# Chunked attention and a squared-ReLU feed-forward on one core: transposes of q, k and of the attention output by DMA instead of by TensorE

## The chip, the cores and the metric

The kernel runs on one core of a Trainium2 chip. A core has five engines with a queue of instructions each: TensorE (PE, with its weight loads as PEld), VectorE (DVE), ScalarE (ACT), GpSimd (POOL) and SyncE (SP), which here issues all DMAs. 16 DMA engines do the transfers. The metric is the device time of one execution in microseconds (us); lower is better.

## The reference

Attention within chunks of 64 tokens, and then a feed-forward layer over all tokens. B = 8, H = 8 heads, S = 576, D = 64, so 4608 tokens of 512 features; d_ff = 2048.

```
q_c, k_c, v_c = (t.reshape(B, H, S // 64, 64, D) for t in (q, k, v))
scores = D ** -0.5 * q_c @ k_c.transpose(0, 1, 2, 4, 3)
attn   = exp(scores - max); attn = attn / (sum(attn) + 1e-09)
x      = (attn @ v_c), heads side by side          # 4608 x 512
h      = maximum(x @ w_in, 0)                       # 4608 x 2048
out    = (h * h) @ w_out                            # 4608 x 512, float32
```

## The kernel before

The tokens are cut into 18 groups of 256, and the groups into 9 blocks: block 0 is groups 0 to 2, blocks 1 to 7 are two groups each (3 and 4, then 5 and 6, up to 15 and 16), block 8 is group 17 alone. q, k and v arrive from HBM as float32; a DMA for q or k brings 128 tokens with 8 heads, in pieces of 256 B. The matmuls take bf16.

For one group the attention has four steps, each a function:

- `transpose_qk` (T): TensorE transposes q (8 pieces of 128x128) and then k (8 more), L139, reading the upper halves of the float32 words as bf16. Both halves lie in one PSUM tile `ps_att`; DVE copies q's half to `qkT` (L146) and ACT copies k's half (L148).
- `scores` (SC): 64 matmuls of two groups (32 of one) at L160, then ACT's exponential (L167).
- `values` (AV): matmuls with v and a column of ones (L179); DVE takes the reciprocal of the sums (L186) and writes the normalized `x` in bf16 (L189), 128 tokens at a time.
- `transpose_x` (XT): TensorE transposes x (8 pieces, L205) and DVE copies the result to `xT` (L209).

`ffn_in` has 16 steps for a block: four matmuls (L224) into a bank of `ps_ffn`, ACT's relu (L230), DVE's square into `gT` (L231). `ffn_out` has 16 matmuls (L240) for each 128 tokens, ACT's copy to one of four `o_sb` buffers (L247) and a store (L249). `ps_ffn` has four banks and `ps_att` two.

The order is written by hand. The feed-forward of block j yields after each step of `ffn_in` and after every fourth matmul of `ffn_out`; each yield is a slot, 32 in a block of two groups. A plan puts the attention of block j+1 in slots of block j: T in slots 1 and 4, SC of both groups in 9, AV in 14 and 18, XT in 22 and 26. The loads of block j+2 (L85 for q and k, L97 and L104 for v) are issued on SP at the start of block j. Every queue runs in this order, so an instruction that waits on SP holds all later loads and stores.

Of the kernel before, what the change touches and what calls it, by code (L numbers as in the profile page):

```python
# [10 lines left out]
BF16 = mybir.dt.bfloat16  # L11
# [5 lines left out]
def kernel(  # L17
# [9 lines left out]
    nc = tc.nc  # L27

    B, H, S, D = q.shape
# [4 lines left out]
    n_hp = H // 2  # L34
    n_dt = d_model // 128
    n_ft = d_ff // 128
    GT = 256
    n_grp = n_tokens // GT
    blocks = [[0, 1, 2]] + [[g, g + 1] for g in range(3, n_grp - 1, 2)] + [[n_grp - 1]]
    BT = GT * max(len(b) for b in blocks)  # L40

    const_pool = ctx.enter_context(tc.tile_pool(name="const", bufs=1))
# [3 lines left out]
    att_pool = ctx.enter_context(tc.tile_pool(name="att", bufs=3))  # L46
# [20 lines left out]
    def segments(g0, n):  # L67
        while n:
            b, s = divmod(g0, S)
            m = min(n, S - s)  # L70
            yield b, s, m
            g0 += m
            n -= m

    qk = {}

    def load_qk(g):
        q_sb = in_pool.tile([128, 2, H, D], FP32, name="q_sb")
        k_sb = in_pool.tile([128, 2, H, D], FP32, name="k_sb")
        qk[g] = (q_sb, k_sb)  # L80
        for t in range(2):
            for dst, src in ((q_sb, q), (k_sb, k)):
                p = 0
                for b, s, m in segments(g * GT + t * 128, 128):
                    nc.sync.dma_start(  # L85
                        out=dst[p:p + m, t, :, :],
                        in_=src[b, :, s:s + m, :].rearrange("h s d -> s h d"))
                    p += m
# [19 lines left out]
    def load_w_in(i):  # L108
        cols = slice(i * 256, (i + 1) * 256)
        st = wst_pool.tile([128, 1024], FP32, name="w_st").rearrange("p (a f) -> p a f", a=n_dt)  # L110
        nc.sync.dma_start(  # L111
            out=st, in_=moe_w_in[:, cols].rearrange("(a p) f -> p a f", p=128))
        nc.gpsimd.tensor_copy(out=w_in_bf[:, :, cols], in_=st)  # L113
# [8 lines left out]
    xTs = {}  # L122
# [4 lines left out]
    state = {}  # L127

    def transpose_qk(g):
        ps = ps_att.tile([128, 1024], FP32, name="ps_att")  # L130
        psb = ps.bitcast(BF16)
        qkT = att_pool.tile([128, 2, n_hp, GT], BF16, name="qkT")
        state["qkT", g] = qkT
        for which in range(2):
            srcb = qk[g][which].bitcast(BF16)
            for hp in range(n_hp):
                for i in range(2):
                    c0 = which * 1024 + hp * GT + i * 128
                    nc.tensor.transpose(  # L139
                        out=psb[:, c0:c0 + 128],  # L140
                        in_=srcb[:, i, 2 * hp:2 * hp + 2, 1::2],
                        identity=ident)
            dst = qkT[:, which]
            src = psb[:, which * 1024:(which + 1) * 1024].rearrange("c (h t) -> c h t", h=n_hp)
            if which == 0:
                nc.vector.tensor_copy(out=dst, in_=src)  # L146
            else:
                nc.scalar.copy(out=dst, in_=src)  # L148

    def scores(g):  # L150
        qkT = state.pop(("qkT", g))
        ps = ps_att.tile([128, 1024], FP32, name="ps_att")
        for hp in range(n_hp):
            for t in range(2):
                for a in range(2):
                    for p in range(2):
                        c = p ^ a
                        cols = slice(t * 128 + p * 64, t * 128 + p * 64 + 64)
                        o0 = a * 512 + hp * 128 + t * 64
                        nc.tensor.matmul(  # L160
                            out=ps[64 * c:64 * c + 64, o0:o0 + 64],
                            lhsT=qkT[64 * a:64 * a + 64, 1, hp, cols],
                            rhs=qkT[64 * a:64 * a + 64, 0, hp, cols],
                            start=True, stop=True)
        e = att_pool.tile([128, 2, n_hp, 2, 64], BF16, name="e")
        state["e", g] = e
        nc.scalar.activation(  # L167
            out=e.rearrange("p a h t q -> p (a h t q)"), in_=ps, func=AF.Exp, scale=scale)
# [26 lines left out]
    def transpose_x(g):  # L195
        j, c = place[g]
        if j not in xTs:
            xTs[j] = att_pool.tile([128, n_dt, BT], BF16, name="xT", bufs=2)
        ps = ps_att.tile([128, 1024], FP32, name="ps_att")
        psb = ps.bitcast(BF16)  # L200
        for t in range(2):
            x = state.pop(("x", g, t))
            for hp in range(n_hp):
                c0 = hp * GT + t * 128
                nc.tensor.transpose(  # L205
                    out=psb[:, c0:c0 + 128],
                    in_=x[:, hp].rearrange("p a d -> p (a d)"),
                    identity=ident)
        nc.vector.tensor_copy(  # L209
            out=xTs[j][:, :, c:c + GT],  # L210
            in_=psb[:, 0:1024].rearrange("p (h t) -> p h t", h=n_hp))

    T, SC, AV, XT = transpose_qk, scores, values, transpose_x

    gTs = {}

    def ffn_in(j, c, n):
        if j not in gTs:
            gTs[j] = ffn_pool.tile([128, n_ft, BT], BF16, name="gT")
        gT, xT = gTs[j], xTs[j]  # L220
        for ft in range(n_ft):
            h = ps_ffn.tile([128, 512], FP32, name="ps_ffn")
            for dt in range(n_dt):
                nc.tensor.matmul(  # L224
                    out=h[:, 0:n],
                    lhsT=w_in_bf[:, dt, ft * 128:(ft + 1) * 128],
                    rhs=xT[:, dt, c:c + n],
                    start=(dt == 0), stop=(dt == n_dt - 1))
            rl = ffn_pool.tile([128, 512], BF16, name="rl", bufs=3)
            nc.scalar.activation(out=rl[:, 0:n], in_=h[:, 0:n], func=AF.Relu)  # L230
            nc.vector.tensor_tensor(  # L231
                out=gT[:, ft, c:c + n], in0=rl[:, 0:n], in1=rl[:, 0:n], op=ALU.mult)
            yield

    def ffn_out(j):
        gT = gTs.pop(j)
        for tt in range(len(blocks[j]) * GT // 128):
            o_ps = ps_ffn.tile([128, d_model], FP32, name="ps_ffn")
            for ft in range(n_ft):
                nc.tensor.matmul(  # L240
                    out=o_ps,
                    lhsT=gT[:, ft, tt * 128:(tt + 1) * 128],
                    rhs=w_out_bf[:, ft, :],
                    start=(ft == 0), stop=(ft == n_ft - 1))
                if ft == n_ft - 1:
                    o_sb = ffn_pool.tile([128, d_model], FP32, name="o_sb", bufs=4)
                    nc.scalar.copy(out=o_sb, in_=o_ps)  # L247
                    t0 = blocks[j][0] * GT + tt * 128
                    nc.sync.dma_start(out=out[t0:t0 + 128, :], in_=o_sb)  # L249
                if ft % 4 == 3:  # L250
                    yield

    def load(g):
        load_qk(g)
        load_v(g)

    load(0)
    load(1)
    load_w_in(0)
    load_w_in(1)  # L260
    load(2)
    for i in range(2, 8):
# [10 lines left out]
    for j, grps in enumerate(blocks):  # L273
        if j + 2 < len(blocks):
            for g in blocks[j + 2]:
                load(g)
        nxt = blocks[j + 1] if j + 1 < len(blocks) else []
        if j == 0:
            a, b = nxt
            plan = {3: [(T, 2)], 6: [(SC, 2)], 10: [(AV, 2)], 14: [(XT, 2)],  # L280
                    44: [(T, a)], 46: [(T, b)], 48: [(SC, a), (SC, b)],
                    50: [(AV, a)], 52: [(AV, b)], 54: [(XT, a)], 55: [(XT, b)]}
            phases = [ffn_in(0, 0, 512), ffn_in(0, 512, 256), ffn_out(0)]
        else:
            if len(nxt) == 2:
                a, b = nxt
                plan = {1: [(T, a)], 4: [(T, b)], 9: [(SC, a), (SC, b)], 14: [(AV, a)],
                        18: [(AV, b)], 22: [(XT, a)], 26: [(XT, b)]}
            elif nxt:
                a, = nxt  # L290
                plan = {1: [(T, a)], 6: [(SC, a)], 14: [(AV, a)], 20: [(XT, a)]}
            else:
                plan = {}
            phases = [ffn_in(j, 0, len(grps) * GT), ffn_out(j)]
        slot = 0
        for phase in phases:
            for _ in phase:
                for f, g in plan.get(slot, []):
                    f(g)
                slot += 1  # L300
# [30 lines left out]
```

## Time and profile before

| | |
|---|---|
| median of 3 runs | 353.45 us (352.02 to 353.71) |
| the profiled execution: its own time | 352.24 us |
| its span | 350.2 us |
| PE busy | 303.3 us, 87% |
| ACT busy | 142.7 us, 41% |
| DVE busy | 120.7 us, 34% |
| GpSimd busy | 18.6 us, 5%, all of it before the 60th us |
| chain that ended last | PE 78%, SP's queue 8%, DVE 6%, ACT 3% |

The profile records one execution. A span of an engine is busy when an instruction executes; times of issuing a DMA are listed for SP's queue (SPq) but not counted as busy. The chain that ended last is followed back from the last instruction, at each step to what released it. A DMA share is the mean busy share of the 16 DMA engines. The granted clock is the share of TensorE's full speed that the chip allowed in a stretch.

### The profile page before, as it was taken

What the parts mean: (1) busy time and instruction counts of PE and PEld (TensorE: products, weight loads), DVE (VectorE), ACT (ScalarE), POOL (GpSimd) and SP (SyncE); (2) the same over time, 40 slices, a digit from 0 to 9 for tenths busy, and PEclk for the clock granted to TensorE, in tenths of its full rate; (3) what the DMA queues carried; (4) which work ended last, traced back from release to release, by engine and by line L of the source; (5) the groups of instructions that cost most, each with busy time, mean ns of one, the idle gap of its engine ahead of it and who ended that gap; (6) DMA issues with size and microseconds to landing.
All of it is one profiled execution on the core that took longest, in us unless ns stands there. A gap on an engine that the chain in (4) does not pass through costs nothing.

```text
span 350.2 us, 6792 instructions
## 1 busy us (share of the span) xinstructions
PE 303.3 (87%) x2800; PEld 157.9 (45%) x2800; DVE 120.7 (34%) x268; ACT 142.7 (41%) x233; POOL 18.6 (5%) x28
## 2 busy tenths in 40 slices
PE   2456979989589988998899889988998899899995
PEld 1322447444244544454445444544454445444472
DVE  0322395015235314531453145314531453144050
ACT  0323545250455146514651465146514651473171
POOL 1021681000000000000000000000000000000000
PEclk9999899999699999999999999999999999999999
DMA  9997998998992159414861586159615601100101
GB/s 168 193 229 217 366 362 179 200 172 172 278 187 48 60 140 199 85 62 117 183 122 62 135 168 121 63 136 171 115 62 138 104 2 60 62 0 31 60 32 60
DMA packets 125278, 46.58 MB, mean 133 GB/s; under 512 B 114496, under 2 KB 118592, under 8 KB 125248
## 3 DMA queue, kind: packets, MB, share of 16 engines
q1 hardware_dynamic: 125248, 46.15, 56.9%
q8 instruction: 22, 0.36, 0.5%
q14 instruction: 8, 0.07, 0.1%
HBM read 36.70 MB, written 9.44 MB: 132 GB/s over the span
## 4 chain that ended last, share of the span: by engine, by line
PE 78%; SPq 8%; DVE 6%; ACT 3%; DMA 2%; issue 1%; POOL 0%; ACTq 0%
PE ps_ffn L240 36%; PE ps_ffn L224 35%; SPq L85 3%; PE ps_att L139 3%; DVE gT L231 3%; DVE qkT L146 3%; ACT rl L230 3%; SPq L104 2%; PE ps_att L205 2%; SPq L97 2%; PE ps_att L179 2%; PE ps_att L160 2%; DMA w_st<-in_moe_w_in_dram 1%; DMA out_dram<-o_sb 1%; SPq L111 1%
## 5 line engine op out<-in xcount | busy, mean ns | idle before, releaser
L224 PE MATMUL ps_ffn<-xT,w_in_bf 128*128 128x512 bf16 (+1 forms) x640 | 137.5, 369 | 6.1 <-DVE xT L209 4.0
L240 PE MATMUL ps_ffn<-w_out_bf,gT 128*128 128x512 bf16 x576 | 130.0, 379 | 0.0
L231 DVE TENSOR_TENSOR gT<-rl 128x512 bf16<-128x512 bf16 (+1 forms) x160 | 68.0, 428 | 136.2 <-ACT rl L230 131.6
L230 ACT ACTIVATE rl<-ps_ffn 128x512 bf16<-128x512 f32 (+1 forms) x160 | 87.5, 557 | 45.2 <-PE ps_ffn L224 42.7
L224 PEld LDWEIGHTS <-w_in_bf 128*128 128x128 bf16 x640 | 62.0, 100 | 66.1 <-issue 8.8
L240 PEld LDWEIGHTS <-gT 128*128 128x128 bf16 x576 | 55.0, 98 | 62.0
L247 ACT COPY o_sb<-ps_ffn 128x512 f32<-128x512 f32 x36 | 21.1, 586 | 113.4 <-PE ps_ffn L240 103.7
L139 PE MATMUL ps_att<-ident,k_sb 128*128 128x128 bf16 x144 | 12.2, 233 | 23.9 <-DVE qkT L146 23.9
L148 ACT COPY qkT<-ps_att 128x1024 bf16<-128x1024 bf16 x18 | 18.2, 1012 | 35.5 <-PE ps_att L139 35.5
L209 DVE COPY xT<-ps_att 128x1024 bf16<-128x1024 bf16 x18 | 12.4, 691 | 38.7 <-PE ps_att L205 38.7
L189 DVE TENSOR_TENSOR x<-ps_att,rec 128x512 bf16<-128x512 f32 x36 | 24.9, 692 | 1.2
L139 PEld LDWEIGHTS <-k_sb 128*128 128x128 bf16 x144 | 10.5, 104 | 26.3 <-issue 15.7
L146 DVE COPY qkT<-ps_att 128x1024 bf16<-128x1024 bf16 x18 | 12.3, 686 | 21.4 <-PE ps_att L139 21.4
L167 ACT ACTIVATE e<-ps_att 128x1024 bf16<-128x1024 f32 x18 | 17.6, 1023 | 2.1 <-PE ps_att L160 2.1
L139 PE MATMUL ps_att<-ident,q_sb 128*128 128x128 bf16 x144 | 12.0, 229 | 6.2 <-DMA q_sb<-in_q_dram 6.2
L139 PEld LDWEIGHTS <-q_sb 128*128 128x128 bf16 x144 | 10.2, 103 | 10.3 <-DMA q_sb<-in_q_dram 6.3
L186 DVE RECIPROCAL rec<-ps_att 128x8 f32<-128x8 f32 x36 | 7.2, 201 | 22.0 <-PE ps_att L179 22.0
L205 PE MATMUL ps_att<-ident,x 128*128 128x128 bf16 x144 | 12.2, 229 | 2.2 <-DVE x L189 2.2
L205 PEld LDWEIGHTS <-x 128*128 128x128 bf16 x144 | 9.9, 101 | 6.8 <-DVE x L189 3.0
L179 PEld LDWEIGHTS <-e 64*64 64x64 bf16 x576 | 6.5, 111 | 9.3 <-issue 5.5
L179 PE MATMUL ps_att<-v_sb,e 64*64 64x65 bf16 x576 | 8.6, 200 | 2.3 <-ACT e L167 2.3
L113 POOL CAST w_in_bf<-w_st 128x1024 bf16<-128x1024 f32 x8 | 8.8, 1096 | 32.7 <-DMA w_st<-in_moe_w_in_dram 32.7
(12 smaller groups left out, 24.6 us busy)
## 6 DMA issues: line engine op xcount, KB each, us to landing
out_dram<-o_sb SPq DMA_DIRECT2D x36, 256.0 KB, 2.0
q_sb<-in_q_dram SPq DMA_DIRECT2D x32, 256.0 KB, 4.3
k_sb<-in_k_dram SPq DMA_DIRECT2D x32, 256.0 KB, 4.8
v_sb<-in_v_dram SPq DMA_DIRECT2D x80, 64.0 KB, 3.0
v_sb<-in_v_dram SPq DMA_DIRECT2D x32, 128.0 KB, 4.5
w_st<-in_moe_w_in_dram SPq DMA_DIRECT2D x8, 512.0 KB, 5.7
w_st<-in_moe_w_out_dram SPq DMA_DIRECT2D x8, 512.0 KB, 6.3
q_sb<-in_q_dram SPq DMA_DIRECT2D x8, 128.0 KB, 3.6
```

Source lines behind the costliest of these rows:

```text
L139: nc.tensor.transpose(out=psb[:, c0:c0 + 128], in_=srcb[:, i, 2 * hp:2 * hp + 2, 1::2], identity=ident)
L146: nc.vector.tensor_copy(out=dst, in_=src)
L148: nc.scalar.copy(out=dst, in_=src)
L167: nc.scalar.activation(out=e.rearrange("p a h t q -> p (a h t q)"), in_=ps, func=AF.Exp, scale=scale)
L179: nc.tensor.matmul(out=ps[64 * p:64 * p + 64, a, hp * (D + 1):(hp + 1) * (D + 1)], lhsT=e[64 * c:64 * c + 64, a, hp, t, :], rhs=vb[64 * c: ...
L189: nc.vector.tensor_tensor(out=x.rearrange("p h a d -> p a h d"), in0=o[:, :, :, 0:D], in1=rec.to_broadcast([128, 2, n_hp, D]), op=ALU.mult)
L205: nc.tensor.transpose(out=psb[:, c0:c0 + 128], in_=x[:, hp].rearrange("p a d -> p (a d)"), identity=ident)
L224: nc.tensor.matmul(out=h[:, 0:n], lhsT=w_in_bf[:, dt, ft * 128:(ft + 1) * 128], rhs=xT[:, dt, c:c + n], start=(dt == 0), stop=(dt == n_dt ...
L230: nc.scalar.activation(out=rl[:, 0:n], in_=h[:, 0:n], func=AF.Relu)
L231: nc.vector.tensor_tensor(out=gT[:, ft, c:c + n], in0=rl[:, 0:n], in1=rl[:, 0:n], op=ALU.mult)
L240: nc.tensor.matmul(out=o_ps, lhsT=gT[:, ft, tt * 128:(tt + 1) * 128], rhs=w_out_bf[:, ft, :], start=(ft == 0), stop=(ft == n_ft - 1))
L247: nc.scalar.copy(out=o_sb, in_=o_ps)
```

## The change

From group 5 on, q and k are no longer transposed on TensorE. GpSimd casts both to one bf16 tile `qkb` of 128x2048, and one transposing DMA on SP writes `qkT`; this new step is called CT. It is in the plan two blocks ahead, in the last slots of block j for block j+2 (24 and 27; 48 and 51 in block 0). The output of those groups goes to `xT` by two transposing DMAs, issued right behind the group's values. SC moves from slot 9 to slot 6. Groups 0 to 4 stay on TensorE, but T now transposes q and k before either is copied. The layout of `qkT` has the 128-token half ahead of the head pair. At the start, group 1's q and k are loaded ahead of group 0's v, and the first weight piece ahead of group 1's v.

```
+    FIRST_DMA_X = 5
...
+    def cast_transpose_qk(g):
+        qkb = att_pool.tile([128, 2, 2 * H * D], BF16, name="qkb", bufs=2)
+        for which in range(2):
+            nc.gpsimd.tensor_copy(
+                out=qkb[:, which], in_=qk[g][which].rearrange("p t h d -> p (t h d)"))
+        qkT = att_pool.tile([128, 2, 2, n_hp, 128], BF16, name="qkT", bufs=4)
+        state["qkT", g] = qkT
+        nc.sync.dma_start_transpose(
+            out=qkT.rearrange("c w t h q -> c (w t h) q"),
+            in_=qkb.rearrange("p w c -> p (w c)"))
...
+        if g >= FIRST_DMA_X:
+            for t in range(2):
+                x = state.pop(("x", g, t))
+                nc.sync.dma_start_transpose(
+                    out=xTs[j][:, :, c + t * 128:c + (t + 1) * 128],
+                    in_=x.rearrange("p h a d -> p (h a d)"))
+            return
...
-    load(0)
-    load(1)
+    load_qk(0)
+    load_qk(1)
+    load_v(0)
     load_w_in(0)
+    load_v(1)
     load_w_in(1)
...
-                plan = {1: [(T, a)], 4: [(T, b)], 9: [(SC, a), (SC, b)], 14: [(AV, a)],
-                        18: [(AV, b)], 22: [(XT, a)], 26: [(XT, b)]}
+                plan = {6: [(SC, a), (SC, b)], 14: [(AV, a), (XT, a)],
+                        18: [(AV, b), (XT, b)]}
...
+        far = blocks[j + 2] if j + 2 < len(blocks) else []
+        last = sum(16 if i + 1 < len(phases) else 2 * len(grps) * 4 for i in range(len(phases)))
+        for i, g in enumerate(far):
+            plan.setdefault(last - 8 + 3 * i, []).append((CT, g))
```

SP's order in one of the repeating blocks, before: the end of the loads, the block's four stores, and the first loads of the next block.

```order
L97 DMA v_sb_94<-in_v_dram 128x4x64
L104 DMA v_sb_94<-in_v_dram 64x4x64 x2
L249 DMA out_dram<-o_sb 128x512 x4
L85 DMA q_sb<-in_q_dram 128x8x64
L85 DMA k_sb<-in_k_dram 128x8x64
```

The same place now. The names are x and qkb for the sources, xT and qkT for the transposed tiles.

```order
L98 DMA v_sb_92<-in_v_dram 128x4x64
L105 DMA v_sb_92<-in_v_dram 64x4x64 x2
L215 DMA_TRANSPOSE xT<-x 128x4x128 x4
L269 DMA out_dram<-o_sb 128x512 x2
L159 DMA_TRANSPOSE qkT<-qkb 128x16x128
L269 DMA out_dram<-o_sb 128x512
L159 DMA_TRANSPOSE qkT<-qkb 128x16x128
L269 DMA out_dram<-o_sb 128x512
L86 DMA q_sb<-in_q_dram 128x8x64
```

Six transposing DMAs have come between the loads and the next block's loads, and they are mixed with the stores.

ACT's order over one such block, before: relu of two steps, k's copy, relu of three, k's copy, and so on.

```order
L230 ACTIVATE rl<-ps_ffn 128x512 x2
L148 COPY qkT<-ps_att 128x1024
L230 ACTIVATE rl<-ps_ffn 128x512 x3
L148 COPY qkT<-ps_att 128x1024
L230 ACTIVATE rl<-ps_ffn 128x512 x5
L167 ACTIVATE e<-ps_att 128x1024 x2
L230 ACTIVATE rl<-ps_ffn 128x512 x6
L247 COPY o_sb<-ps_ffn 128x512 x4
```

The same block now.

```order
L250 ACTIVATE rl<-ps_ffn 128x512 x7
L180 ACTIVATE e<-ps_att 128x1024 x2
L250 ACTIVATE rl<-ps_ffn 128x512 x9
L267 COPY o_sb<-ps_ffn 128x512 x4
```

Both copies of k are gone, and the exponentials stand behind the seventh relu instead of the tenth.

## Rows read from the trace of the kernel before

**Rows 1.** Table of stages (start:end us, length, busy us of each engine, PEclk, DMA share, GB/s)

```profile
85.80:125.90 40.10, 35.20 (x305) 17.25 (x305) 12.62 (x28) 15.77 (x25) 0.00 (x0) 0.91 0.58 142
125.90:161.00 35.10, 32.44 (x306) 16.39 (x305) 12.62 (x28) 15.29 (x24) 0.00 (x0) 1.00 0.57 121
```

**Rows 2.** PE's timeline of block 2 (start us, length us, engine, line, operation)

```profile
125.87 1.89 PE L224 MATMUL ps_ffn<-xT,w_in_bf 128*128 128x512 bf16 x8
127.60 0.61 PE L139 MATMUL ps_att<-ident,q_sb 128*128 128x128 bf16 x8
...
129.95 2.75 PE L224 MATMUL ps_ffn<-xT,w_in_bf 128*128 128x512 bf16 x12
132.54 0.61 PE L139 MATMUL ps_att<-ident,q_sb 128*128 128x128 bf16 x8
...
134.95 4.48 PE L224 MATMUL ps_ffn<-xT,w_in_bf 128*128 128x512 bf16 x20
...
148.37 0.45 PE L179 MATMUL ps_att<-v_sb,e 64*64 64x65 bf16 x32
...
152.22 0.61 PE L205 MATMUL ps_att<-ident,x 128*128 128x128 bf16 x8
152.67 3.62 PE L240 MATMUL ps_ffn<-w_out_bf,gT 128*128 128x512 bf16 x16
...
160.88 1.46 PE L224 MATMUL ps_ffn<-xT,w_in_bf 128*128 128x512 bf16 x6
```

**Rows 3.** Timeline of all engines, end of block 0 and start of block 1

```profile
85.71 4.20 SPq L249 DMA_DIRECT2D out_dram<-o_sb  x6
85.78 1.89 PE L224 MATMUL ps_ffn<-xT,w_in_bf 128*128 128x512 bf16 x8 [0.78 <-DVE xT L209]
...
87.50 0.61 PE L139 MATMUL ps_att<-ident,q_sb 128*128 128x128 bf16 x8
...
88.17 0.59 ACT L247 COPY o_sb<-ps_ffn 128x512 f32<-128x512 f32 x1 [9.46 <-PE ps_att L139]
...
91.65 1.01 PE L139 MATMUL ps_att<-ident,k_sb 128*128 128x128 bf16 x8 [3.54 <-DVE qkT L146]
...
92.46 5.18 PE L224 MATMUL ps_ffn<-xT,w_in_bf 128*128 128x512 bf16 x12
```

**Rows 4.** Chain that ended last, same place (start us, length us, what)

```profile
85.02 0.60 SPq L104
...
86.35 2.51 DMA out_dram<-o_sb
```

**Rows 5.** PE's timeline, group 3's transposes in block 0

```profile
70.44 0.61 PE L139 MATMUL ps_att<-ident,k_sb 128*128 128x128 bf16 x8 [0.78 <-DVE qkT L146]
```

**Rows 6.** Groups by line (operation and count | busy us, mean ns | idle before, releaser)

```profile
L189 DVE TENSOR_TENSOR x<-ps_att,rec 128x512 bf16<-128x512 f32 x36 | 24.9, 692 | 1.2
...
L113 POOL CAST w_in_bf<-w_st 128x1024 bf16<-128x1024 f32 x8 | 8.8, 1096 | 32.7 <-DMA w_st<-in_moe_w_in_dram 32.7
...
L186 DVE RECIPROCAL rec<-ps_att 128x8 f32<-128x8 f32 x36 | 7.2, 201 | 22.0 <-PE ps_att L179 22.0
```

**Rows 7.** SP's queue in block 2: first load, last k load, last v loads

```profile
127.07 0.43 SPq L85 DMA_DIRECT2D q_sb<-in_q_dram  x1
...
137.15 1.07 SPq L85 DMA_DIRECT2D k_sb<-in_k_dram  x1
...
141.68 1.97 SPq L104 DMA_DIRECT2D v_sb<-in_v_dram  x2
```

**Rows 8.** Table of stages, the loads of block 2 and its stores

```profile
127.10:143.70 16.60, 13.94 (x150) 7.39 (x148) 6.57 (x15) 11.02 (x18) 0.00 (x0) 1.00 1.06 202
...
150.00:162.00 12.00, 12.00 (x70) 5.92 (x68) 1.96 (x3) 2.23 (x5) 0.00 (x0) 1.00 0.18 67
```

**Rows 9.** DMA issues (operation and count, KB each, median us from issue to landing)

```profile
k_sb<-in_k_dram SPq DMA_DIRECT2D x32, 256.0 KB, 4.8
v_sb<-in_v_dram SPq DMA_DIRECT2D x80, 64.0 KB, 3.0
```

More of the change, by code (lines that the diff above doesn't have):

```diff
@@ L131, in transpose_qk @@
         psb = ps.bitcast(BF16)
-        qkT = att_pool.tile([128, 2, n_hp, GT], BF16, name="qkT")
+        qkT = att_pool.tile([128, 2, 2, n_hp, 128], BF16, name="qkT", bufs=4)
         state["qkT", g] = qkT
@@ L137, in transpose_qk @@
                 for i in range(2):
-                    c0 = which * 1024 + hp * GT + i * 128
+                    c0 = which * 1024 + i * 512 + hp * 128
                     nc.tensor.transpose(
@@ L142, in transpose_qk @@
                         identity=ident)
-            dst = qkT[:, which]
-            src = psb[:, which * 1024:(which + 1) * 1024].rearrange("c (h t) -> c h t", h=n_hp)
+        for which in range(2):
+            dst = qkT[:, which].rearrange("c t h q -> c (t h q)")
+            src = psb[:, which * 1024:(which + 1) * 1024]
             if which == 0:
@@ L148, in transpose_qk @@
                 nc.scalar.copy(out=dst, in_=src)
+    def cast_transpose_qk(g):
+        qkb = att_pool.tile([128, 2, 2 * H * D], BF16, name="qkb", bufs=2)
+        for which in range(2):
+            nc.gpsimd.tensor_copy(
+                out=qkb[:, which], in_=qk[g][which].rearrange("p t h d -> p (t h d)"))
+        qkT = att_pool.tile([128, 2, 2, n_hp, 128], BF16, name="qkT", bufs=4)
+        state["qkT", g] = qkT
+        nc.sync.dma_start_transpose(
+            out=qkT.rearrange("c w t h q -> c (w t h) q"),
+            in_=qkb.rearrange("p w c -> p (w c)"))
     def scores(g):
@@ L157, in scores @@
                         c = p ^ a
-                        cols = slice(t * 128 + p * 64, t * 128 + p * 64 + 64)
+                        cols = slice(p * 64, p * 64 + 64)
                         o0 = a * 512 + hp * 128 + t * 64
@@ L161, in scores @@
                             out=ps[64 * c:64 * c + 64, o0:o0 + 64],
-                            lhsT=qkT[64 * a:64 * a + 64, 1, hp, cols],
-                            rhs=qkT[64 * a:64 * a + 64, 0, hp, cols],
+                            lhsT=qkT[64 * a:64 * a + 64, 1, t, hp, cols],
+                            rhs=qkT[64 * a:64 * a + 64, 0, t, hp, cols],
                             start=True, stop=True)
@@ L211, in transpose_x @@
             in_=psb[:, 0:1024].rearrange("p (h t) -> p h t", h=n_hp))
-    T, SC, AV, XT = transpose_qk, scores, values, transpose_x
+    T, CT, SC, AV, XT = transpose_qk, cast_transpose_qk, scores, values, transpose_x
     gTs = {}
@@ L286 @@
                 a, b = nxt
-                plan = {1: [(T, a)], 4: [(T, b)], 9: [(SC, a), (SC, b)], 14: [(AV, a)],
-                        18: [(AV, b)], 22: [(XT, a)], 26: [(XT, b)]}
+                plan = {6: [(SC, a), (SC, b)], 14: [(AV, a), (XT, a)],
+                        18: [(AV, b), (XT, b)]}
             elif nxt:
                 a, = nxt
-                plan = {1: [(T, a)], 6: [(SC, a)], 14: [(AV, a)], 20: [(XT, a)]}
+                plan = {6: [(SC, a)], 14: [(AV, a), (XT, a)]}
             else:
```

## The prediction

> **What bounds the kernel now.** I read the table of stages first, then PE's timeline of one repeating block, then the timeline and the chain of waits around 86 us, then SP's queue beside the DMA shares, and last the durations by line. The table shows a block of two groups (512 tokens): 35.1 us at granted clock 1.00, PE busy 32.44, ACT 15.29, DVE 12.62, GpSimd nothing, DMA share 0.57 [rows 1]. Five such blocks (2 to 6) follow block 1, which takes 40.1 us at clock 0.91. So from about 90 us on PE sets the pace, and what leaves PE's order there leaves the time, if nothing else comes late.
>
> PE's timeline of block 2 has the change's targets with their waits [rows 2]. From L224 at 125.87 to the same place at 160.88 a block takes 35.01 us. The q transposes start at 127.60, and the next L224 matmul only at 129.95: 2.35 us, of which the matmuls are the smaller part, since the k half waits for DVE's copy of the q half. The second group costs 132.54 to 134.95, 2.41 us. The output transposes cost 152.22 to 152.67, 0.45 us, and the same again for the second group. That is 5.66 us a block; without them 29.35 us is left.
>
> Block 1 starts with a fault of another kind. SP is still issuing loads at 85 us, which is where the chain passes through it [rows 4], and the six stores queued behind them are issued from 85.71 on, 4.20 us for six [rows 3]. The first lands at 88.86 (86.35 + 2.51, [rows 4]). ACT has four o_sb buffers, so the last two of its six copies (the first of them at 88.17) wait for stores to land, and behind them in ACT's order wait the relu, then on DVE the square and the copy that lets k's transposes go. PE does L224 x8 at 85.78, then q's transposes, and then stands until 91.65. After that stand, 12 matmuls are 5.18 us instead of 2.75 [rows 2, 3]: the lower of the two clock levels.
>
> **The change, part by part.** All durations are of the one profiled execution: span 350.2 us, its time 352.24, so 2.0 us lie around the span; the median of the runs shown is 353.45, 1.2 above that execution.
>
> *Transposes leave PE (groups 5 to 17).* Blocks 2 to 6: five times 5.66 = 28.3 us. Block 7 prepares one group, with the same pattern: 2.35 + 0.45 = 2.8 us. Where a stall goes, the next in line are the ps_ffn banks, which ACT empties with 0.6 us of relu for each 0.86 us of PE work; ACT loses two 1 us copies a block and its 15.29 us stand in 29.35, so I cost that at nothing.
>
> *Groups 0 to 4 stay on PE, both halves before the copies.* For groups 3 and 4 this takes away the wait of k's half, 0.78 us each [rows 5], but ahead of the stand at 86 us, so it only lengthens the stand: nothing. The earlier groups sit in front of weights that land late, and the same number of DMA issues stands ahead of the third weight piece as before: nothing, within 1 us either way.
>
> *Block 1.* SP's loads of groups 5 and 6 still end near 85.6 us, so the stores do not come sooner, and the ps_ffn bank that PE needs for the third L224 group becomes free when the first late copy is done, 88.17 + 0.59 = 88.8. From there 29.35 less the two L224 groups already done (85.78 to 87.50, 1.72) = 27.6 us are left, and 2.8 us for the half clock (5.18 - 2.75, and 1.01 - 0.61 in the k transposes at 91.65), which I keep since PE again stands some 3 us. Block 1 ends at 119.2 instead of 125.87: 6.7 us saved, between 3.9 (as long a stand as before) and 9.5 (no loss of clock).
>
> *Casts on GpSimd.* Two casts of 128x1024 a group at 1096 ns [rows 6], 4.4 us a block on an engine without work there. The last k load of a block is issued at 138.2, 12.4 us into it [rows 7], and lands 4.8 us later [rows 9]; the casts are done near 20 us, ahead of the transposing DMAs in slots 24 and 27 (a slot is four matmuls, 0.86 us). Nothing.
>
> *The new DMAs.* A block issues two of 128x2048 and four of 128x512 elements on SP. The trace shows no such operation, so I bound it. Counted in rows of 256 B they are 2 x 2048 + 4 x 512, over 16 DMA engines 384 each per block. The loads give the nearest price: in the 16.6 us in which they run the share is 1.06 [rows 8], 17.6 us for 12288 packets of 256 B, 768 per engine: 22.9 ns each. At that price the transposes take 8.8 us. Below: four stores, 1.05 MB, in 0.18 x 12 = 2.2 us [rows 8], by which 1.57 MB take 3.3 us. Above: each 128x128 piece by itself, at one DMA issue (0.6 us, [rows 4]) or one small DMA's landing (3.0 us, [rows 9]): 48 pieces a block, 29 or 144 us. I take 8.8, since the row size and the engines are the same. Loads and stores hold 0.57 x 35.1 = 20.0 us already, which makes 28.8 of 29.35: hidden, but barely. The Trainium skill ("DMA: Bandwidth & Descriptors", section "Latency and other measured facts") has a measured 261 GB/s for a DMA transpose. By it the block's 1.57 MB would take an estimated 6.0 us, 26.0 in all, and the time would be the same with more room; no run shown here has such a DMA.
>
> *SP's order.* Behind each block's loads (127.07 to 143.65, [rows 7]) now stand the four output transposes, two stores, a q/k transpose, a store, a q/k transpose, a store, and then the next block's loads. A wait on a cast or on x holds all of it. Values of the second group start at 148.37, 12.5 us ahead of the block's end [rows 2]; reciprocals and x take DVE 2 x (0.69 + 0.20) = 1.8 us [rows 6], four issues at 0.7 another 2.8, and a 256 KB load's landing 4.8: 3.1 us to spare. The second q/k transpose has 11 slots, 9.5 us, to the scores that need it, less about 1.5 for the store ahead: 8 us against the same 4.8. SP's sum is 16.6 + 4 x 0.7 + 6 x 0.7 = 23.6 of 29.35. Nothing, with 3 us of room.
>
> Sum: 28.3 + 2.8 + 6.7 = 37.8 us; 352.24 - 37.8 = 314.4, and by the median 315.6. I say 316.
>
> **Rivals.** *A: the DMA engines set the block.* For it: 28.8 of 29.35 leaves no room, and SP's order packs loads and transposes in series. Against: a share of 0.18 in the last third of a block [rows 8], where the transposes come. If a row costs 31 ns, a third over a load's packet, a block is 20.0 + 12.0 = 32.0; blocks 1 to 5 carry two groups' transposes, so 5 x 2.65 = 13 us come back: 329.
>
> *B: a transpose runs as a series of 128x128 pieces, and SP holds for them (slower).* For it: SP is in order, and more than half of a block is its loads. The price is one issue, 0.6 us, per piece: 48 x 0.6 = 28.8 us on top of 16.6 + 2.8, a block of 48.2, and 316 + 5 x 18.9 = 410. It decides from 0.36 us a piece, where a block takes 36.9 us and the 37.8 us are used up. Against: each transpose is one instruction on SP. The Trainium skill ("VectorE: DVE Perf Modes", section "The three transpose paths") gives 1309 ns for a 128x128 by DMA and 390 for TensorE. The trace has 0.45/8 us = 56 ns a piece on PE in a run of eight [rows 2], so PE is cheaper here than the page makes it. With 1309 ns in series the estimate is 63 us for a block's pieces and some 580 in all.
>
> *C: a row costs the DMA engines two packets (slower).* One to fetch it, one to scatter it: 45.8 ns x 384 = 17.6, a block of 37.6, 316 + 5 x 8.3 = 357. It turns slower from 44 ns a row. For it: the elements of a transposed row go to 128 different partitions. Against: nothing in the trace.
>
> *D: no change.* Another chain of 35 us a block would be needed; ACT, DVE, the DMAs and SP all stand well below [rows 1, 7].
>
> **How the numbers follow.** Forecast 0.60, A 0.16, D 0.03, B 0.11, C 0.10. A measurement of this kernel tells about 0.5%, 1.8 us, from no change; so faster is 0.60 + 0.16 less a little for A's far end = 0.75, same 0.03, slower 0.22. The forecast's own range is 308 (no loss of clock in block 1, and some of the stand gone) to 324 (1.6 us a block late). A and half of C are needed for 8 in 10: the range ends at 366. B, C's upper half and 0.03 below are left out.
>
> **What would show it.** The forecast: blocks 2 to 6 last 29.4 us, PE runs L224's and L240's matmuls with only scores and values between, and the stand near 86 us ends near 88.8. A: PE waits for xT or qkT that a DMA writes, blocks of 30 to 34 us, DMA share above 0.9 all through. B: SP held far over 1 us by a transpose, loads starting late in a block, and PE waiting for them. C: a DMA share near 1 with SP free. What makes me wrong is a transposing DMA dearer than 44 ns a row, or a hold of several us on SP at each; a block 1 that ends at 125 again would cost 6 us and leave the sign.

## The result, and the profile after

The changed kernel takes 328.58 us (median of 4 runs, 326.71 to 330.25) against 352.96 for the kernel before on the same chip: a ratio of 0.931, with a 95% interval of 0.925 to 0.937. It is faster, as forecast, and inside the whole range of 308 to 366, but past the forecast's own range of 308 to 324; the point value of 316 was 12.6 us too low. The profiled execution took 328.05 us, its span is 326.3. In `e7_both` below, two of the four executions fell into a slower state of the chip, and its time is that of the other two.

First PE's own order. In this timeline (start, length, engine, line, operation, and in brackets the wait just ahead and its releaser) L244 is the first half of the feed-forward, L173 are the scores, L260 is the second half.

```profile
81.69 1.89 PE L244 MATMUL ps_ffn<-xT,w_in_bf 128*128 128x512 bf16 x8 [0.78 <-DVE xT L229]
88.87 5.82 PE L244 MATMUL ps_ffn<-xT,w_in_bf 128*128 128x512 bf16 x19 [5.29 <-ACT o_sb L267]
...
96.75 0.45 PE L173 MATMUL ps_att<-qkT 64*64 64x64 bf16 x32 [1.68 <-DMA qkT<-qkb]
...
120.02 6.20 PE L244 MATMUL ps_ffn<-xT,w_in_bf 128*128 128x512 bf16 x27 [0.16 <-DMA xT<-x]
126.15 0.44 PE L173 MATMUL ps_att<-qkT 64*64 64x64 bf16 x32
127.93 0.44 PE L173 MATMUL ps_att<-qkT 64*64 64x64 bf16 x32 [1.33 <-DMA qkT<-qkb]
128.30 7.08 PE L244 MATMUL ps_ffn<-xT,w_in_bf 128*128 128x512 bf16 x31
...
151.66 4.69 PE L244 MATMUL ps_ffn<-xT,w_in_bf 128*128 128x512 bf16 x20 [0.62 <-ACT o_sb L267]
...
279.49 6.21 PE L244 MATMUL ps_ffn<-xT,w_in_bf 128*128 128x512 bf16 x27
```

The transposes of [rows 2] are gone from the repeating blocks, and three waits have come instead: the second group's scores for their transposing DMA (1.33 us here), the block's first matmul for `xT` (0.16) or for the bank that ACT empties into `o_sb` (0.62). Block 2 is 151.66 - 120.02 = 31.6 us, and blocks 2 to 6 together (to the first L244 of block 7 at 279.49) are 159.5, 31.9 each on the mean, where before they were 35.0 and the forecast said 29.35.

The table of stages answers to [rows 1] and [rows 8]: blocks 1, 2, 3 and 6, and then three stretches of SP's work: block 2's loads, four output transposes, and the q/k transposes that follow them with stores between.

```profile
81.70:120.00 38.30, 30.97 (x252) 13.85 (x256) 11.11 (x24) 14.24 (x24) 6.24 (x6) 0.96 0.86 185
120.00:151.60 31.60, 29.48 (x252) 13.56 (x256) 11.09 (x24) 14.17 (x23) 4.16 (x4) 1.00 0.85 183
151.60:183.60 32.00, 29.48 (x252) 13.57 (x257) 10.99 (x24) 13.81 (x23) 4.32 (x4) 1.00 0.88 184
248.40:279.50 31.10, 30.67 (x253) 14.03 (x258) 10.88 (x24) 12.85 (x21) 2.44 (x2) 0.95 0.77 177
126.60:145.20 18.60, 17.12 (x167) 8.12 (x171) 8.54 (x18) 8.66 (x14) 3.56 (x4) 1.00 0.89 185
145.20:150.40 5.20, 5.20 (x26) 2.35 (x24) 0.00 (x0) 0.58 (x1) 0.60 (x1) 1.00 0.51 106
151.50:158.00 6.50, 6.29 (x51) 2.88 (x56) 2.46 (x6) 3.85 (x8) 0.00 (x0) 1.00 1.07 250
```

PE is busy 29.48 of 31.60 us. No other engine is near its limit, and the DMA share is 0.85, up from 0.57: high, but not full. In the output transposes it is 0.51: half of the DMA engines' time is unused while PE will soon wait for what they bring. In the q/k transposes it is 1.07: there the engines are full.

SP's queue tells why. From one block's output transposes (L215) to the next block's (the long stretch of loads left out):

```profile
113.50 5.17 SPq L215 DMA_TRANSPOSE xT<-x  x4
118.77 1.00 SPq L269 DMA_DIRECT2D out_dram<-o_sb  x2
119.87 2.86 SPq L159 DMA_TRANSPOSE qkT<-qkb  x1
122.82 0.53 SPq L269 DMA_DIRECT2D out_dram<-o_sb  x1
123.45 1.91 SPq L159 DMA_TRANSPOSE qkT<-qkb  x1
125.45 1.09 SPq L269 DMA_DIRECT2D out_dram<-o_sb  x1
126.59 0.43 SPq L86 DMA_DIRECT2D q_sb<-in_q_dram  x1
...
143.81 1.29 SPq L105 DMA_DIRECT2D v_sb<-in_v_dram  x2
145.20 5.17 SPq L215 DMA_TRANSPOSE xT<-x  x4
```

SP issues without a pause for 31.7 us (113.50 to 145.20), and so in the next blocks: L215 comes again at 176.98, 208.26 and 241.98, periods of 31.8, 31.3 and 33.7. Each row begins when the one before it has ended, so each holds SP for its length, and SP waits for no data in between (semaphore waits of 17 ns in the median at L215, L159 and L269): the transposes 5.17 + 2.86 + 1.91 = 9.9 us, the stores 2.6, the loads 18.6, and 0.5 lies between. Before, the loads were 16.6 us of a 35 us block [rows 7, 8], and besides them SP had only four stores. Block 6 is another case: only one group is left to load, and L215 comes 24.1 us later, at 266.09. What its 31.04 us have over 29.35 is mostly the lower clock after a wait of 2.08 us just ahead of it: 0.95 in the table, with PE busy 30.67 us instead of 29.48. The profile names no releaser for that wait; the last output transpose of block 5 was issued near 245.9 and would land about then. How long one transpose holds SP and when it lands, `xT`'s first (ns and us, minimum/median/maximum):

```profile
L215 SPq DMA_TRANSPOSE xT<-x x26: 1190/1217/1662, 113.5 to 296.4; - x26
...
DMA to landing us min/median/max: 2.4/2.5/4.1
```

The same view of `qkT`:

```profile
L159 SPq DMA_TRANSPOSE qkT<-qkb x13: 1905/2697/3659, 87.8 to 273.8; - x13
...
DMA to landing us min/median/max: 4.4/4.6/4.7
```

The price on the DMA engines comes from the page of the profile. The kernel before (packets; then the queue's packets, MB, share of 16 engines' span):

```profile
DMA packets 125278, 46.58 MB, mean 133 GB/s; under 512 B 114496, under 2 KB 118592, under 8 KB 125248
...
q1 hardware_dynamic: 125248, 46.15, 56.9%
```

The kernel after, with its chain that ended last and one of the new casts:

```profile
DMA packets 166461, 56.77 MB, mean 174 GB/s; under 512 B 155680, under 2 KB 159776, under 8 KB 166432
...
q1 hardware_dynamic: 166432, 56.38, 76.5%
...
PE 58%; SPq 23%; DMA 14%; issue 3%; ACT 1%; POOL 1%; DVE 0%
...
L155 POOL CAST qkb<-q_sb 128x1024 bf16<-128x1024 f32 x13 | 13.9, 1070 | 177.0 <-DMA q_sb<-in_q_dram 155.2
```

13 transposes of 2048 rows and 26 of 512 are 39936 rows of 256 B; of packets under 512 B there are 41184 more, so a row is one packet (the other 1248 would be 32 for each transpose). If loads and stores took what they took before, the rows are the difference: the queue's time went from 0.569 x 350.2 = 199.3 to 0.765 x 326.3 = 249.6 us: 50.4 us for 39936 / 16 = 2496 rows per engine, 20.2 ns a row. The chain has moved: SP's queue was 8% of it and is 23%, the DMAs another 14%.

### The profile page after: what moved, and what is told of

It is laid out like the page before. It is cut to its first block, busy times and chain, and to the rows that moved or that the text cites. A ratio compares the mean times of both kernels' runs of the same rounds, so it can differ in the third digit from the quotient of the medians.

```text
span 326.3 us, 6239 instructions
## 1 busy us (share of the span) xinstructions
PE 281.8 (86%) x2452; PEld 139.6 (43%) x2488; DVE 111.2 (34%) x242; ACT 131.4 (40%) x220; POOL 46.2 (14%) x54
## 4 chain that ended last, share of the span: by engine, by line
PE 58%; SPq 23%; DMA 14%; issue 3%; ACT 1%; POOL 1%; DVE 0%
PE ps_ffn L260 29%; PE ps_ffn L244 25%; DMA qkT<-qkb 7%; SPq L86 7%; SPq L105 4%; SPq L215 3%; SPq L159 3%; SPq L98 3%; DMA w_st<-in_moe_w_out_dram 2%; DMA w_st<-in_moe_w_in_dram 2%; PE ps_att L192 2%; SPq L269 2%; DMA xT<-x 1%; PE ps_att L173 1%; DMA v_sb<-in_v_dram 1%
## 5 line engine op out<-in xcount | busy, mean ns | idle before, releaser
L244 PE MATMUL ps_ffn<-xT,w_in_bf 128*128 128x512 bf16 (+1 forms) x616 | 132.5, 366 | 16.8 <-ACT o_sb L267 5.9
L251 DVE TENSOR_TENSOR gT<-rl 128x512 bf16<-128x512 bf16 (+1 forms) x160 | 75.1, 477 | 159.8 <-ACT rl L250 156.3
L260 PE MATMUL ps_ffn<-w_out_bf,gT 128*128 128x512 bf16 x564 | 126.7, 379 | 0.9 <-issue 0.3
L244 PEld LDWEIGHTS <-w_in_bf 128*128 128x128 bf16 x640 | 62.0, 100 | 79.1 <-issue 19.6
L260 PEld LDWEIGHTS <-gT 128*128 128x128 bf16 x576 | 55.5, 98 | 65.4 <-ACT rl L250 0.4
L155 POOL CAST qkb<-q_sb 128x1024 bf16<-128x1024 f32 x13 | 13.9, 1070 | 177.0 <-DMA q_sb<-in_q_dram 155.2
L173 PE MATMUL ps_att<-qkT 64*64 64x64 bf16 x576 | 8.1, 200 | 10.6 <-DMA qkT<-qkb 6.9
L155 POOL CAST qkb<-k_sb 128x1024 bf16<-128x1024 f32 x13 | 13.7, 1054 | 5.4 <-DMA k_sb<-in_k_dram 5.1
L114 POOL CAST w_in_bf<-w_st 128x1024 bf16<-128x1024 f32 x8 | 8.7, 1084 | 32.8 <-DMA w_st<-in_moe_w_in_dram 32.8
L150 ACT COPY qkT<-ps_att 128x1024 bf16<-128x1024 bf16 x5 | 5.1, 1012 | 19.5 <-DVE qkT L148 19.5
L173 PEld LDWEIGHTS <-qkT 64*64 64x64 bf16 x576 | 6.2, 113 | 15.5 <-DMA qkT<-qkb 7.5
L148 DVE COPY qkT<-ps_att 128x1024 bf16<-128x1024 bf16 x5 | 3.5, 690 | 22.8 <-PE ps_att L140 22.8
L140 PE MATMUL ps_att<-ident,q_sb 128*128 128x128 bf16 x40 | 4.1, 256 | 6.2 <-DMA q_sb<-in_q_dram 6.2
L121 POOL CAST w_out_bf<-w_st 128x1024 bf16<-128x1024 f32 x8 | 8.7, 1091 | 2.5 <-DMA w_st<-in_moe_w_out_dram 2.5
L140 PEld LDWEIGHTS <-q_sb 128*128 128x128 bf16 x40 | 3.3, 116 | 7.1 <-DMA q_sb<-in_q_dram 6.3
```

What stands on the lines that cost most here:

```text
L155: nc.gpsimd.tensor_copy(out=qkb[:, which], in_=qk[g][which].rearrange("p t h d -> p (t h d)"))
L173: nc.tensor.matmul(out=ps[64 * c:64 * c + 64, o0:o0 + 64], lhsT=qkT[64 * a:64 * a + 64, 1, t, hp, cols], rhs=qkT[64 * a:64 * a + 64, 0, t, ...
L244: nc.tensor.matmul(out=h[:, 0:n], lhsT=w_in_bf[:, dt, ft * 128:(ft + 1) * 128], rhs=xT[:, dt, c:c + n], start=(dt == 0), stop=(dt == n_dt ...
L251: nc.vector.tensor_tensor(out=gT[:, ft, c:c + n], in0=rl[:, 0:n], in1=rl[:, 0:n], op=ALU.mult)
L260: nc.tensor.matmul(out=o_ps, lhsT=gT[:, ft, tt * 128:(tt + 1) * 128], rhs=w_out_bf[:, ft, :], start=(ft == 0), stop=(ft == n_ft - 1))
```

## The experiments

Theory S: SP's in-order issuing sets blocks 2 to 6, since its holds add up to more than PE's 29.35 us. Rival D: the 16 DMA engines set them. All kernels are the changed one with the edit shown.

**Stores issued from ACT's queue** (`e1_stores_act`).

```
-                    nc.sync.dma_start(out=out[t0:t0 + 128, :], in_=o_sb)
+                    nc.scalar.dma_start(out=out[t0:t0 + 128, :], in_=o_sb)
```

> The changed kernel with the output stores issued on ACT's queue, right behind ACT's own copy, instead of on SP's. Theory S (SP's in-order queue sets blocks 2 to 6: loads 18.6 + four output transposes 5.2 + two q/k transposes 4.8 + four stores 2.5 with gaps = 31.7 us, the period measured): SP falls to 29.2, PE's 29.35 sets the block, 29.4 to 29.9 us each, five times 2 us less; the stand of PE from 83.6 to 88.9 goes too, since the copies no longer wait for stores that stand behind loads on SP. About 312 us (309 to 317). Rival D (the 16 DMA engines set the block, share 0.85 to 0.88, and SP's long issues are their backpressure): the DMAs are the same, so blocks stay at 31.5 us or more and only the stand goes: 322 to 326 us.

Measured 327.48 us (ratio 0.928, 0.919 to 0.938): no gain that can be told, and a miss for both, but the trace shows a gain and two losses. Without stores between them the two q/k transposes of blocks 2 to 6 took 4.75 to 6.14 us of SP, against 4.8 to 5.5 in the changed kernel, and some loads were held longer; SP's period became 30.5, 32.0, 29.1 and 32.8 us. Blocks 2, 3, 5 and 6 are 31.4, 30.3, 29.4 and 31.2 us, 1.4 less on the mean than in the changed kernel. What that gave was lost elsewhere. The stand in block 1 didn't go but moved to the first scores, so that block 2 began at 124.22 instead of 120.02:

```profile
96.43 0.65 PE L173 MATMUL ps_att<-qkT 64*64 64x64 bf16 x32 [5.79 <-DMA qkT<-qkb]
```

And ACT got a wait of its own at the start of block 4, which became 35.0 us (all engines' timeline; ACTq is ACT's DMA queue):

```profile
184.56 5.83 SPq L159 DMA_TRANSPOSE qkT<-qkb  x2
...
192.30 0.34 ACTq L269 DMA_DIRECT2D out_dram<-o_sb  x1
...
192.74 2.60 ACT L250 ACTIVATE rl<-ps_ffn 128x512 bf16<-128x512 f32 x5 [6.90 <-DMA qkT<-qkb]
```

ACT stood 6.9 us, released when a transposing DMA landed that it has no use for. The built program has both queues' DMAs take turns on eight completion semaphores, and ahead of the store at 192.30 ACT waits for the one that the second of SP's two q/k transposes raises. The chain agrees: that transpose's transfer ends at 192.22, and the store is issued 0.08 us later.

**A shorter v** (`e2_short_v`): the v loads of groups 5 and up bring 2 of the 8 heads, in the same number of DMAs.

```
+        hv = H if g < 5 else 2
...
-                    in_=v[b, 0::2, s:s + m, :].rearrange("h s d -> s h d"))
+                    in_=v[b, 0:hv:2, s:s + m, :].rearrange("h s d -> s h d"))
```

> The changed kernel, but from group 5 on the v loads fetch 2 of the 8 heads (the others keep old values, so the output is not the reference's): as many DMA issues on SP, 3072 packets of 256 B fewer a block, 192 per engine, 4.4 us of the DMA engines at 22.9 ns. Theory S with holds that are fixed per issue: nothing changes, 31.7 us a block, 328. Rival D: blocks fall to PE's 29.4 us, 316 to 318. A mixture (SP's holds contain backpressure of the engines) also falls to about 29.4; then the loads' stretch on SP must fall from 18.6 to near 20 x 0.65 = 13 us.

Measured 323.19 us (0.918, 0.909 to 0.927). Blocks 2 to 6 are 31.0 us on the mean, 0.9 less, and the DMA share fell to 0.74 to 0.78. That is 0.85 x 31.6 - 0.78 x 30.2 = 3.3 us less engine work in block 2 and 5.2 in block 3, for 0.9 us of time: less than D's gain and more than S's nothing. SP's loads became 0.4 to 1.3 us shorter, and SP's period with them (30.4, 31.3, 30.2 and 32.8 us). Part of that is the short loads' own hold: a pair at L106 mostly holds SP 1.11 us where it held 1.29, and a block has four. So the run doesn't show that a hold contains work that the engines still have ahead; block 2's q/k transposes held SP as long as before, 2.85 and 1.90 us.

**Four tiny DMAs a block** (`e3_tiny_dmas`): 4 KB each, on SP behind the loads.

```
+            if j >= 1:
+                for i in range(4):
+                    nc.sync.dma_start(
+                        out=tiny[:, (4 * j + i) * D:(4 * j + i + 1) * D], in_=q[0, 0, 0:16, :])
```

> The changed kernel with four loads of 16 rows of 256 B added on SP behind each block's loads, from block 1 on: 64 packets a block, 0.1 us of the DMA engines, but four more issues of 0.6 us. Theory S: blocks 2 to 6 grow by 2.4 to 2.6 us, 34.2 each, and the time to about 340 us. Rival D: at most 0.3 us a block, 328 to 330.

Measured 339.07 us (0.963, 0.953 to 0.974), where S expected about 340. SP's queue, and below it the stages of blocks 2 and 3:

```profile
148.44 1.98 SPq L302 DMA_DIRECT2D tiny<-in_q_dram  x4
150.53 5.17 SPq L216 DMA_TRANSPOSE xT<-x  x4
```

```profile
123.10:157.00 33.90, 31.12 (x257) 13.91 (x258) 10.96 (x24) 13.50 (x22) 4.25 (x4) 0.95 0.81 171
157.00:191.50 34.50, 31.18 (x256) 13.85 (x257) 10.98 (x24) 13.45 (x22) 4.26 (x4) 0.95 0.77 170
```

2.0 us of issues with next to no bytes (16 KB beside 3 MB of loads) lengthened these blocks by 2.0 and 2.6 us over the mean of 31.9, while the DMA share fell to 0.8. With engines as the limit it would have stayed. SP's period is 33.9 and 34.5 us here (L216 at 116.62, 150.53 and 185.00), the same as the blocks. PE's clock is lower too, 0.95, but PE still waits 2.8 and 3.3 us for `xT` at the end of these blocks, so the clock is not what sets them.

**One output transpose a group instead of two** (`e5_x_merged`): both halves of `x` in one tile, the same bytes, two issues a block fewer.

```
-            for t in range(2):
-                x = state.pop(("x", g, t))
-                nc.sync.dma_start_transpose(
-                    out=xTs[j][:, :, c + t * 128:c + (t + 1) * 128],
-                    in_=x.rearrange("p h a d -> p (h a d)"))
+            x = state.pop(("x", g))
+            nc.sync.dma_start_transpose(
+                out=xTs[j][:, c // 128:c // 128 + 2].rearrange("c t h q -> c (t h) q"),
+                in_=x.rearrange("p t h a d -> p (t h a d)"))
```

> The changed kernel with the output transposes merged: one DMA of 128x1024 for a group instead of two of 128x512 (x of a group in one tile, xT laid out by 128 tokens), so two issues a block instead of four, with the same bytes and rows. Theory S (SP's order of issues sets the block): a hold between 1.22 us (128x512) and 2.7 us (128x2048), some 1.5, twice, instead of 5.2 us: SP's block falls by about 2.1, blocks 2 to 6 from 31.9 to 29.8 us, the time to 318. Rival D (the DMA engines set it): the same work for them, 31.5 us or more a block, 327 to 329.

Measured 316.25 us (0.900, 0.893 to 0.907), near S's 318 and far from D's 327 to 329. PE's timeline, SP's queue and the stage of block 3:

```profile
120.43 6.21 PE L244 MATMUL ps_ffn<-xT,w_in_bf 128*128 128x512 bf16 x28
...
150.02 6.21 PE L244 MATMUL ps_ffn<-xT,w_in_bf 128*128 128x512 bf16 x28
...
179.37 6.21 PE L244 MATMUL ps_ffn<-xT,w_in_bf 128*128 128x512 bf16 x28
```

```profile
114.99 2.66 SPq L215 DMA_TRANSPOSE xT<-x  x2
...
143.70 2.69 SPq L215 DMA_TRANSPOSE xT<-x  x2
```

```profile
150.00:179.40 29.40, 29.40 (x258) 13.57 (x257) 11.46 (x24) 13.44 (x22) 4.30 (x4) 1.00 0.90 195
```

Twice the size holds SP 1.28 us (median of 13) where the half-size transpose held it 1.22. Two issues fewer take 2.5 us off SP's 31.7, PE becomes the limit at 29.35 to 29.7 and is busy all through, and the DMA engines do the same work in a shorter block at a higher share. They had the room. That settles S against D.

**v loads on GpSimd's queue** (`e6_v_gpsimd`), and this together with the merged transpose (`e7_both`).

```
+        eng = nc.sync if g < 5 else nc.gpsimd
...
-                nc.sync.dma_start(
+                eng.dma_start(
```

> The changed kernel with the v loads of groups 5 and up issued on GpSimd's queue instead of SP's: twelve issues a block leave SP, the bytes stay. Theory S: SP's loads shrink from 18.6 to about 8 x 1.47 = 11.8 us, its block to 25, and PE's 29.35 sets it; the stores ahead of block 1 leave SP sooner too. 313 to 317. Rival D: 31.5 us or more a block, 325 to 329. Open: what an issue costs on GpSimd, which no run so far shows; over 1.5 us each it would delay the casts.

> Merged output transposes and v loads on GpSimd together. Theory S: PE's 29.35 to 29.6 us a block, with some 8 us to spare on SP, so no more than 1 us better than the better of the two alone: 312 to 316. Rival D: 31.5 us or more a block, 325 to 329. This is also the candidate that may beat both kernels.

Measured 328.13 (0.934, 0.926 to 0.942) and 326.0 us (0.928, 0.919 to 0.937): both missed by 10 us or more. In the first, blocks 2, 3, 4 and 6 are 29.35 to 29.44 us, as S has it, but block 1 is 43.5. PE there:

```profile
104.79 0.64 PE L174 MATMUL ps_att<-qkT 64*64 64x64 bf16 x32 [9.24 <-DMA qkT<-qkb]
```

and the landing of `qkT`'s transposes in this kernel:

```profile
DMA to landing us min/median/max: 4.4/6.9/13.9
```

With a second queue at work a transpose lands after 6.9 us instead of 4.6, at worst after 13.9. What SP gains is lost elsewhere: block 2 begins at 130.44, 10.4 us later than after the change, most of it the wait shown (1.68 us after the change) and the lower clock behind it (0.74 from 105.36 to 115.26), and block 5 is 3.6 us over the others. In the second kernel's profiled execution (330.18 us) PE waits 9.68 us for `qkT` at the same place and block 1 is 42.8 us; that the same cause holds for its shorter executions is argued.

**Back on PE, part by part**: output transposes on PE (`e4_x_on_pe`), q and k on PE (`e8_qk_on_pe`), both on PE (`e9_all_on_pe`), where of the change only the new order of T (both halves ahead of the copies), the layout of `qkT` and the order of the first loads are left.

```
-    FIRST_DMA_X = 5
+    FIRST_DMA_X = 99
...
+                plan = {6: [(SC, a), (SC, b)], 14: [(AV, a)], 18: [(AV, b)],
+                        22: [(XT, a)], 26: [(XT, b)]}
```

```
+                plan = {1: [(T, a)], 4: [(T, b)], 9: [(SC, a), (SC, b)],
+                        14: [(AV, a), (XT, a)], 18: [(AV, b), (XT, b)]}
...
-        far = blocks[j + 2] if j + 2 < len(blocks) else []
+        far = []
```

> One part of the change undone: the attention output is transposed on PE again (slots 22 and 26) for all groups, q and k stay with the cast and the DMA. PE gains 0.9 us a block (30.25), SP loses the four output transposes, 5.2 of 31.7. Theory S: PE sets the block at 30.3 us, five times 1.4 less, block 7 0.45 more: 322. Rival D: 2.6 us fewer of the DMA engines a block, also PE's 30.3, 322. If it stays at 328 the q/k transposes alone cost it.

> The other part alone: q and k on PE for all groups (slots 1 and 4, both halves before the copies), the attention output by four DMAs a block as in the change. Theory S: SP carries loads, stores and four output transposes, 16.6 + 2.5 + 5.2 = some 25 us, so PE sets the block: 32.04 as measured with everything on PE, less 0.89 for the output's transposes, 31.15. Five times 0.89 and 0.45 less than with everything on PE: 325. If the transposing DMAs had a price of their own beside the issue on SP (in landing, in what PE waits for), blocks would be 32 us or more.

> All transposes on PE for all groups, no cast and no transposing DMA, in the slots of before; what is left of the change is that the q and k halves are both transposed ahead of the copies, the layout of qkT, and the order of the first loads. Theory: most of what the q/k transposes cost on PE is the wait of k's half for DVE's copy of q's half (2.38 us a group, of which 16 x 56 ns = 0.9 are the transposes), so a block takes 35.01 - 2 x 1.48 = 32.05 us, and the time is 333 to 336, without a single DMA moved. Rival: the wait comes back elsewhere (scores wait for the copies, or the PSUM tile for its turn), 35 us a block and 348 to 352; then the gain of the change is the DMAs' alone.

| q, k by | x by | us | ratio (95%) | block 2 to 6, us |
|---|---|---|---|---|
| PE, new order (e9) | PE | 329.97 | 0.939 (0.932 to 0.947) | 32.04 |
| PE, new order (e8) | DMA | 326.06 | 0.926 (0.916 to 0.936) | 31.14 |
| DMA (e4) | PE | 321.63 | 0.914 (0.905 to 0.922) | 30.28 |
| DMA (the change) | DMA, 4 issues | 328.58 | 0.931 (0.925 to 0.937) | 31.9 |
| DMA (e5) | DMA, 2 issues | 316.25 | 0.900 (0.893 to 0.907) | 29.5 |

In e4, e8 and e9 PE sets the block. The times of e4 and e8 are within 1.1 us of their theory's; e9 is 3 us below its 333 to 336, though its blocks came out at the 32.05 us expected: its block 1 ended at 120.58, 5.3 us before that of the kernel before. Each DMA part alone pays (over e9); together, in four and two issues, they pay less than q and k alone, because only then does SP's sum pass PE's. And the table's first row shows: without a single transposing DMA the kernel is about as fast as with all six. Its PE timeline:

```profile
120.58 1.89 PE L244 MATMUL ps_ffn<-xT,w_in_bf 128*128 128x512 bf16 x8
122.31 0.61 PE L140 MATMUL ps_att<-ident,q_sb 128*128 128x128 bf16 x8
122.76 0.61 PE L140 MATMUL ps_att<-ident,k_sb 128*128 128x128 bf16 x8
123.20 2.75 PE L244 MATMUL ps_ffn<-xT,w_in_bf 128*128 128x512 bf16 x12
```

T costs 123.20 - 122.31 = 0.89 us a group, not the 2.35 of [rows 2]: the wait for DVE's copy of the q half was 1.5 of it, and goes by issuing k's matmuls ahead of the copies.

**The best of it** (`e10_best`): the merged transpose, six `o_sb` buffers, and q and k of groups 5 and 6 on PE.

```
-                    o_sb = ffn_pool.tile([128, d_model], FP32, name="o_sb", bufs=4)
+                    o_sb = ffn_pool.tile([128, d_model], FP32, name="o_sb", bufs=6)
...
+            if j == 1:
+                plan = {1: [(T, a)], 4: [(T, b)], 9: [(SC, a), (SC, b)],
+                        14: [(AV, a), (XT, a)], 18: [(AV, b), (XT, b)]}
```

> Merged output transposes, six o_sb buffers instead of four, and q and k of groups 5 and 6 on PE, so that SP has no transposes beside block 0's stores. Theory: ACT's copies no longer wait for stores that stand behind loads on SP, so PE has no stand near 84 us and no loss of clock after it; block 1 takes 29.4 + 1.8 us for the two groups' transposes and ends near 114.5 instead of 120.4; the other blocks stay at 29.4 to 29.6. About 310 us (308 to 313). Rival: the stand only moves, since the DMA engines are full until 90 us: values of group 6 or the output transposes wait for loads of groups 5 to 8 that come no sooner, block 1 ends at 118 or later, 314 to 317.

Measured 311.06 us (0.882, 0.874 to 0.890; 309.22 to 312.54), faster than both kernels. PE's timeline, blocks 2 and 3:

```profile
113.68 6.21 PE L244 MATMUL ps_ffn<-xT,w_in_bf 128*128 128x512 bf16 x28
...
122.29 0.44 PE L173 MATMUL ps_att<-qkT 64*64 64x64 bf16 x32 [2.03 <-DMA qkT<-qkb]
122.67 8.77 PE L244 MATMUL ps_ffn<-xT,w_in_bf 128*128 128x512 bf16 x32
...
146.94 6.21 PE L244 MATMUL ps_ffn<-xT,w_in_bf 128*128 128x512 bf16 x28
...
176.29 6.21 PE L244 MATMUL ps_ffn<-xT,w_in_bf 128*128 128x512 bf16 x28
```

The stand near 86 us is gone and block 2 begins 6.3 us earlier than after the change; later blocks are 29.35. Block 2 still loses 3.9 us: 2.2 around the wait for the first q/k transposes, and 1.7 in the 32 matmuls behind it (8.77 us at a granted clock of 0.80, 7.08 in the blocks without that wait). Beside e5's 316.25 the six buffers and groups 5 and 6 on PE give 5.2 us together; they were not run apart.

## Why the prediction was right in sign and 12.6 us off

*PE's terms: right.* The 5.66 us a block were there to be had. The merged kernel shows the 29.35 us block, and its time of 316.25 is the forecast's figure. The prediction saw that the matmuls were the smaller part of T's price; what it did not draw from that is that the new order by itself removes the wait for the copy, 1.5 of 2.35 us, in every block (e9).

*Block 1: right where the stand ends, in part by luck where the block ends.* The stand ended at 88.87 (predicted 88.8), block 2 began at 120.02 (119.2). That block 1 starts 4.1 us earlier than before only lengthened the stand, to 5.29 us, as the step had it, though it is more than the 1.6 us named there. In e2 to e5, e8 and e9, which keep as many DMAs ahead of those stores on SP, block 1 begins anywhere from 82.11 to 85.36 and the stand still ends at 89.3 to 90.5. Behind the stand two errors met: the lower clock cost 1.5 us, not 2.8 (PE busy 29.09 us from 88.87 to 120.02, against the 27.6 left at full clock), and the second group's scores waited 1.68 us for a q/k transpose behind SP's stores, which the step did not have.

*Block 7: right.* It takes 28.6 us (279.49 to 308.09); 31.4 less 2.8 was the forecast.

*Casts: right.* 1.07 us each, hidden.

*The DMA engines' price: right.* 22.9 ns a row predicted, 20.2 measured, and "hidden, but barely" held in the merged kernel, at a share of 0.90 to 0.99. The Trainium skill ("DMA: Bandwidth & Descriptors", section "Latency and other measured facts") gives 261 GB/s for a transpose with a non-contiguous middle dimension; 256 B in 20.2 ns on 16 engines are 203 here, with loads and stores beside, and the measurement decides. The 1309 ns that the Trainium skill ("VectorE: DVE Perf Modes", section "The three transpose paths") gives for a 128x128 are not a price in series here: sixteen pieces land in 4.6 us.

*SP's order: wrong.* The step that failed is "SP's sum is 16.6 + 4 x 0.7 + 6 x 0.7 = 23.6 of 29.35. Nothing, with 3 us of room." The sum was the right one to make; its terms were mis-sized. Six transposes hold SP 9.9 us, not 4.2, since a transpose was priced like a plain issue and holds 1.22 us or 2.7; the loads behind them take 18.6, not 16.6; with 0.5 between and stores 0.2 under, SP needs 31.7 us. That is 2.4 above PE's 29.35, not 3 us or more below it, and the blocks came out 2.5 above it: 5 x 2.54 = 12.7 us, of which block 6's 1.7 is mostly the lower clock after the wait ahead of it. With 0.8 in block 1 that is 13.5 of the 13.6 us between 314.4 and the profiled 328.05.

*The rivals.* A gave 329, near the measured time, by another cause. Two of its three signs came true, blocks of 30 to 34 us and PE's waits for `xT` and `qkT`; the third did not, since the share is 0.79 to 0.88 in blocks 2 to 5, not above 0.9, and e3 and e5 rule the engines out as what sets the block. A number that fits is not a mechanism shown. It is also luck that the time lies in the whole range: beyond 324 the range was there for A and C, and neither came true. B named the right place, SP held by transposes, at the wrong price: not 0.6 us a piece but 1.22 for four, 1.28 for eight and about 2.7 for sixteen. C is refuted by the one packet a row.

*Open.* Why a 128x2048 transpose holds SP 1.9 to 3.7 us, and the loads 2 us longer. Work that the DMA engines still have ahead of them would fit e1, where transposes and some loads were held longer once the stores had left SP's queue, but in e2 the engines had less to do and the q/k transposes held SP as long as before.

## What to carry to other kernels

Add up what each DMA holds its issuing queue, like the busy time of an engine, and take a hold never seen in the trace as the dearest term of the range, not as the usual issue; once the sum passes the slowest engine, every queue entry is on the path. Where holds hardly grow with size, merge the transfers before spreading them over queues. Before work is moved off an engine, ask how much of its price there is a wait: reordering alone (of T and of the first loads, e9) gave nearly all of what six DMAs a block gave.

## What the runs showed of the hardware

- A transposing DMA of 128x512 elements holds SP 1.22 us, one of 128x1024 1.28; a plain load or store 0.52 to 0.74 in the median, by kind.
- A transposing DMA of bf16 from SBUF to SBUF counts one packet per source row of 256 B, and a row took 20.2 ns of a DMA engine.
- Loads issued from GpSimd's queue beside SP's made the same transposes land after 6.9 us instead of 4.6. The Trainium skill ("DMA: Bandwidth & Descriptors", section "Rules for kernel authors") says that another issuing engine brings no bandwidth and only saves issue time; here SP's issue time was the bound, it was saved, and the transposes paid for it.
